# A fused convolution and two-product kernel: block 5 of the convolution gets 20 windows instead of 36, its input is loaded later, and rows go out round by round

## The chip, the cores and the metric

The kernel runs on one core of a Trainium2 chip. The metric is the time of one execution in microseconds (us) of the device. TensorE (PE) multiplies, VectorE (DVE) and ScalarE (ACT) move and scale results out of the accumulation banks, GpSimd (POOL) and SyncE (SP) issue DMA transfers, and the weight loads of TensorE are listed as PEld.

## The reference, cut to what matters

Two steps follow each other. The first is a causal convolution with 7 taps along the sequence; each of 8 heads has its own normalised taps and 24 of the 192 channels. The second is a product of two linear maps, followed by two more linear maps that have no nonlinearity between them.

```python
w = exp(weight - max); w = w / (sum(w) + 1e-9)            # [8 heads, 7 taps]
x_pad = concatenate([zeros((8, 6, 192)), x], axis=1)      # x: [8, 3904, 192]
conv[b, s, h, g] = sum_k w[h, k] * x_pad[b, s + k, h, g]
y = conv.reshape(31232, 192)
a, b = y @ w1, y @ w2                                     # [31232, 1024] each
out = ((a * b) @ w3) @ w_out                              # [31232, 192], float32
```

## The kernel before, in words

**Streams and windows.** The 31,232 tokens are cut into two streams of 15,616 tokens (four sequences each), which sit on the two halves of the 128 partitions. Within a stream the convolution works on windows of 58 new tokens (64 with the six that lap over). A sequence has 68 windows, the last one with 18 tokens, so a stream has 272. `SIZES` cuts them into 12 blocks; `FIRST` holds where each begins, `tok(i)` the token at which window i begins.

**The convolution of a block.** `load_x` brings a block's x in with POOL DMAs, as a whole or in two halves (`halves_of`), cast to bf16 on the way. `zero` clears the six rows ahead of a sequence's first window, where a block holds one. `conv(b, h0, nh)` multiplies nh heads by banded matrices (L290) into one pair of accumulation banks and moves the result to the tile `convo` (L311). `store` writes `convo` to the DRAM tile `rows`, in token order, with two DMAs for each run of windows (48 rows and 10 rows of each window) and one for a sequence's short last window (L330, L334).

**Rounds.** The second step works in rounds of 512 tokens of each stream, 31 in all (numbered 0 to 30, the last with 256). `transposes(R)` brings a round's `rows` back as three DMA transposes into the ring `xT` (L363), which has room for four rounds. `send(last)` issues them on SP for all rounds up to `last` whose tokens are stored. `first_product(R)` (L381, L389, L400) computes both linear maps and their elementwise product into `abT`; `second_product(R, r)` (L434, L439, L446) multiplies by `W_sb` and writes the output for one stream.

**W.** `w3` and `w_out` are multiplied once, ahead of everything that uses them: `w3` goes to DRAM as bf16 (L459), comes back through 16 DMA transposes on SP (L463: 8 for each half of its rows), and `w3_product` (L469, L471) makes the 8 parts of `W_sb` from it. Parts 0 to 3 need the transposes of the first half, parts 4 to 7 those of the second half; the last transpose is read last in each of parts 4 to 7.

**The order.** The whole schedule is written out by hand; each engine and queue works through its own list in order. Blocks 0 to 4 (36 windows) are convolved in a prologue, between the first products of rounds 0 to 2. Block 4 is stored by POOL as far as it is still needed. Then POOL issues, in this order: the load of `w_out`, a two-element copy (`pace`, L559) that waits for one of w3's transposes, and the x of blocks 5 and 6 (L119). PE goes on with the first product of round 3, the eight parts of W, and then the groups: four second products for each stream, into which convolutions are put, then four first products, and so on. A group's loop carries p and the block b = 6 + p that it convolves: three heads behind its second product 1, three behind 3 and two behind 7 (the list `at`). In the group p = 0 block 5 is convolved as well, behind the second products 0, 1 and 2. In later groups the next block's x is loaded behind the first and the second of the four first products, again paced by a two-element copy (L588). The outputs of group 0 go out through POOL's queue, those of later groups through SP's. An SP instruction that waits holds all that stand behind it on SP, and the same holds for POOL.

**What is sent when, before.** Block 5 ends at window 72, token 4136, which covers rounds 4 to 7; block 6 ends at token 6224, which covers rounds 8 to 11. So each block is stored a whole group ahead of the group whose rounds need it.

Of the kernel before, what the change touches and what calls it, by code (L numbers as in the profile page):

```python
# [16 lines left out]
def kernel(  # L17
# [10 lines left out]
    nc = tc.nc  # L28

    B, S, D = x.shape  # L30
    H, K = weight.shape
    G = D // H
    DFF = moe_w1.shape[1]
    JT = DFF // 128
# [4 lines left out]
    CH = 512  # L39
    NR = -(-TS // CH)  # L40
    GROUP = 4
# [4 lines left out]
    WB = -(-S // ST)  # L46
    NWIN = (B // NS) * WB
    LAST = S - (WB - 1) * ST
    SIZES = [6, 4, 8, 10, 8] + [36] * 6 + [20]
    assert sum(SIZES) == NWIN  # L50
    NB = len(SIZES)
    FIRST = [sum(SIZES[:b]) for b in range(NB)]
    PROLOGUE_BLOCKS = 6
    EARLY = SIZES[0] * ST
    MAXN = max(SIZES) // 2

    def tok(i):
        return (i // WB) * S + (i % WB) * ST
# [12 lines left out]
    def banks():  # L71
        p = free.pop(0)
        return p, pairs[:, NS * p:NS * p + NS, :]
# [4 lines left out]
    def drained(p):  # L78
        assert p not in free
        free.append(p)  # L80
# [13 lines left out]
    def halves_of(b):  # L94
        n = SIZES[b] // 2
        return [(FIRST[b], 2 * n)] if 2 * n <= MAXN else [(FIRST[b], n), (FIRST[b] + n, n)]
# [46 lines left out]
    pace = const.tile([1, 2], BF16)  # L143
# [31 lines left out]
    for p0 in (0, Q):  # L175
        nc.gpsimd.affine_select(  # L176
            out=diag[p0:p0 + Q], in_=ones[p0:p0 + Q].to_broadcast([Q, Q + PAD]),
# [3 lines left out]
    for r in range(NS):  # L181
        nc.gpsimd.dma_start(out=xb0[Q * r + PAD:Q * r + Q, 0, :],  # L182
                            in_=x_rows[r * TS:r * TS + ST, :])
# [19 lines left out]
    def warm(n):  # L203
# [14 lines left out]
        out=wall, in0=wall, in1=wmax.unsqueeze(2).to_broadcast([1, H, K]), op=ALU.subtract)  # L218
# [5 lines left out]
        out=wrow, in0=wall, in1=wsum.unsqueeze(2).to_broadcast([1, H, K]), op=ALU.mult)  # L224
# [13 lines left out]
    def band_of(h, r):  # L238
        return Aband[Q * r:Q * r + Q, h // 4, (h % 4) // 2, int(h % 2 != r), :]
# [26 lines left out]
    def segments(c0, n):  # L266
        out = []
        while n:
            m = min(n, Q - c0 % Q)
            out.append((c0 // Q, c0 % Q, m))  # L270
            c0, n = c0 + m, n - m
        return out

    def conv(b, h0, nh, evict=None):
        n = SIZES[b] // 2
        if h0 == 0:
            convo_of[b] = work.tile([128, n, NP, NS, Q], BF16, tag="convo", bufs=2, name="convo")
        convo = convo_of[b]
        p, cps = banks()
        wd = nh * G  # L280

        def view(ps, r):
            return cps[ps, r, 0:n * wd].rearrange("p (w g) -> p w g", g=wd)

        for j in range(nh):
            h = h0 + j
            for c in range(2):
                xb, w0 = xb_of[b][c]
                for r in range(NS):
                    nc.tensor.matmul(  # L290
                        view(slice(Q * c, Q * c + Q), r)[:, :, j * G:(j + 1) * G],
                        band_of(h, r),
                        xb[Q * r:Q * r + Q, w0:w0 + n, h * G:(h + 1) * G],
                        start=True, stop=True)
        src = cps[:, :, 0:n * wd].rearrange("p r (w g) -> p r w g", g=wd)
        o, moves = 0, []
        for k, c0, m in segments(h0 * G, wd):
            moves.append((convo[:, :, k, :, c0:c0 + m].rearrange("p w r g -> p r w g"),
                          src[:, :, :, o:o + m]))
            o += m  # L300
        if h0 + nh == H:
            del xb_of[b]
        if evict == ():
            return p, moves
        if evict == "streams":
            assert nh == H
            return p, [(convo[:, :, :, r, :], src[:, r].rearrange("p w (k g) -> p w k g", k=NP))
                       for r in range(NS)]
        for e, (dst, part) in enumerate(moves):
            f = evict or [nc.scalar.copy]  # L310
            f[e % len(f)](out=dst, in_=part)  # L311
        drained(p)

    stored, sent = [0], [GROUP]

    def store(b, first=0, last=NWIN, queue=nc.sync):
        n = SIZES[b] // 2
        last = min(last, FIRST[b] + 2 * n)
        stored[0] = tok(last) if last < NWIN else TS
        convo = convo_of[b]  # L320
        for c in range(2):
            i0 = FIRST[b] + c * n
            w, end = max(0, first - i0), min(n, last - i0)
            while w < end:
                left = WB - 1 - (i0 + w) % WB
                m = min(end - w, max(1, left))
                src = convo[Q * c:Q * c + ST, w:w + m].rearrange("s w k r g -> s w (k r g)")
                j0 = tok(i0 + w)
                if left == 0:
                    queue.dma_start(out=rows[j0:j0 + LAST, :], in_=src[0:LAST, 0, :])  # L330
                else:
                    dst = rows[j0:j0 + ST * m, :].rearrange("(w s) c -> s w c", s=ST)
                    for s0, s1 in ((0, 48), (48, ST)):
                        queue.dma_start(out=dst[s0:s1], in_=src[s0:s1])  # L334
                w += m
# [23 lines left out]
    def transposes(R, first=0):  # L359
        t0, t1 = max(R * CH, first), min((R + 1) * CH, TS)  # L360
        a = t0 % RING
        for k in range(NP):
            nc.sync.dma_start_transpose(  # L363
                out=xT[k][:, a:a + t1 - t0], in_=rows[t0:t1, k * 128:(k + 1) * 128])
# [45 lines left out]
    def first_product(R, between=None, fts=range(JT), behind_conv=False):  # L410
        if R not in abT_of:
            first_tile(R)
        N = width(R)
        step = CH // N
        for ft in fts[::step]:
            first_part(R, list(range(ft, ft + step)), 0, N)
            if behind_conv and ft == step:
                free[1], free[2] = free[2], free[1]
            if between and ft in between:
                between[ft]()  # L420
# [34 lines left out]
    w3T = const.tile([128, JT, DFF], BF16)  # L455
# [19 lines left out]
    V, A, P = nc.vector.tensor_copy, nc.scalar.copy, nc.gpsimd.tensor_copy  # L475
# [58 lines left out]
    w3_transposes(0, range(JT))  # L534

    def need(R):
        return next(i for i in range(NWIN) if tok(i) >= (R + 1) * CH)

    def send(last):
        while sent[0] <= min(last, NR - 1) and min((sent[0] + 1) * CH, TS) <= stored[0]:  # L540
            transposes(sent[0])
            sent[0] += 1
# [12 lines left out]
        0: seq([(conv, 4, 4, 4)]),  # L555
        3: seq([(pe_transposes, 4)])})
    store(4, need(GROUP - 1) - 1, queue=nc.gpsimd)
    nc.gpsimd.dma_start(out=wo_b, in_=wor)
    P(out=pace, in_=w3T[0:1, 1, DFF - 2:DFF])  # L559
    load_x(5)  # L560
    load_x(6)
    first_product(3)
# [1 line left out]
    def zero(b):  # L564
        for xb, r, w in zero_rows.pop(b, []):
            nc.gpsimd.memset(xb[Q * r:Q * r + PAD, w, :], 0.0)

    def conv_heads(b, heads, f=(nc.vector.tensor_copy,), first=None):
        for j, h in enumerate(heads):
            conv(b, h, 1, (f[j % len(f)],))  # L570
        if heads[-1] == H - 1:
            store(b) if first is None else (store(b, last=first), send(NR), store(b, first))

    slots = (range(0, 3), range(3, 6), range(6, H))
    zero(5)
# [5 lines left out]
    for p, rounds in enumerate(groups):  # L581
        b = PROLOGUE_BLOCKS + p
        order = rounds[-1:] + rounds[:-1] if rounds[-1] == NR - 1 else rounds
        for j, R in enumerate(order if p else ()):
            first_product(R, behind_conv=j == 0 and b <= NB)
            send(R + GROUP)
            if j < 2 and b < NB:
                P(out=pace, in_=abT_of[R][0:1, JT - 1, 1, 0:2])  # L588
                load_x(b, (j,))
        if b < NB:  # L590
            zero(b)
        at = {1: [(b, slots[0])], 3: [(b, slots[1])], 7: [(b, slots[2], (V, A))]}
        if p == 0:
            at = {0: [(5, slots[0], (V, A))], 1: [(5, slots[1], (V, A))],
                  2: [(5, slots[2], (V, A), need(GROUP))], 4: at[1], 5: at[3], 7: at[7]}
        for i, (R, r) in enumerate((R, r) for R in rounds for r in range(NS)):
            second_product(R, r, R == NR - 1 and r == 1, nc.sync if p else nc.gpsimd)
            for c in at.get(i, ()) if b < NB else ():
                conv_heads(*c)
            if p == 0 and i == 2:  # L600
                send(2 * GROUP - 1)
    assert sent[0] == NR


# [28 lines left out]
```

## Time and profile before

| What | Value |
|---|---|
| Median of three runs | 520.85 us (520.66 to 522.95) |
| The profiled execution's own time | 522.15 us |
| Its span, first to last instruction | 520.4 us |
| Mean granted TensorE clock | 0.999 |
| PE busy | 512.2 us, 98% |
| DVE, ACT, POOL busy | 351.9, 330.0, 58.5 us |
| PE on first products (L381) | 3000 matmuls, 319.7 us |
| PE on second products (L434) | 1952 matmuls, 165.0 us |
| PE on the convolution (L290) | 384 matmuls, 17.0 us |
| Moved by DMA | 64.61 MB, mean 124 GB/s |

The busy time of a group is the time in which at least one of its instructions ran; matmuls overlap, so a mean duration times a count is more than the busy time. Idle time stands with the instruction that follows it and what released that instruction. The chain of waits is followed back from the last instruction, at each step to what released it. A DMA's time to landing runs from its issue until its semaphore has been raised in full.

### The profile page before, as it was taken

Reading aid. Unit: us, or ns where it says so; the run is one execution under the profiler, and the core shown is the slowest. Engines: PE = TensorE matmul, PEld = TensorE weight load, DVE = VectorE, ACT = ScalarE, POOL = GpSimd, SP = SyncE. Lnnn points to the kernel's source line nnn. Section 1 sums busy time; section 2 is a strip of 40 time slices with the busy share of each in tenths; the row PEclk is TensorE's granted clock in tenths of the full one; section 3 lists DMA queues with packets and bytes.
Section 4 is the critical chain, followed back from the end, with each engine's and each line's share of the span. In section 5 each row is a group of like instructions: output and inputs, shape, how many; then the busy total and the mean of one; then the engine's idle time right before and its main releaser. Section 6 shows DMA issues by size and latency. Waiting matters only on the chain.

```text
span 520.4 us, 13019 instructions
## 1 busy us (share of the span) xinstructions
PE 512.2 (98%) x5576; PEld 338.0 (65%) x5576; DVE 351.9 (68%) x337; ACT 330.0 (63%) x416; POOL 58.5 (11%) x98
## 2 busy tenths in 40 slices
PE   8999899999999999999999999999999999999997
PEld 4455688445894458845588455884558845599566
DVE  6778644899528995289952899438993199911970
ACT  6887553877438774387743777447774477734762
POOL 8503422030000200003000020001200000000000
PEclk9999999999999999999999999999999999999999
DMA  9979998799747963479644796447824441024004
GB/s 120 165 145 116 153 220 226 158 185 160 141 146 169 115 98 104 141 174 126 85 110 135 167 121 94 116 130 174 104 44 123 139 111 32 17 97 148 2 3 152
DMA packets 133420, 64.61 MB, mean 124 GB/s; under 512 B 90304, under 2 KB 132642, under 8 KB 133298
## 3 DMA queue, kind: packets, MB, share of 16 engines
q1 hardware_dynamic: 94320, 44.06, 36.5%
q0 software_dynamic: 38896, 19.62, 29.0%
q8 instruction: 43, 0.70, 0.6%
q14 instruction: 15, 0.12, 0.1%
q10 hardware_dynamic: 146, 0.10, 0.1%
HBM read 33.25 MB, written 36.52 MB: 134 GB/s over the span
## 4 chain that ended last, share of the span: by engine, by line
PE 87%; SPq 5%; DMA 4%; POOL 3%; issue 0%; ACT 0%; DVE 0%; ACTq 0%
PE pairs L381 53%; PE pairs L434 31%; SPq L463 5%; PE pairs L290 2%; DMA w3rows<-in_moe_w_dram 2%; DMA w3T<-w3rows 2%; POOL xb L119 1%; POOL wd L169 1%; POOL wd L190 1%; PE pairs L469 0%; DMA wall<-in_weight_dram 0%; POOL xb L182 0%; POOL wd L186 0%; POOL xb L172 0%; POOL diag L176 0%
## 5 line engine op out<-in xcount | busy, mean ns | idle before, releaser
L400 DVE TENSOR_TENSOR abT<-asb,pairs 128x1024 bf16<-128x1024 bf16 (+1 forms) x245 | 297.9, 1217 | 52.3 <-ACT asb L389 36.2
L381 PE MATMUL pairs<-xT,wd 64*128 64x512 bf16 (+3 forms) x3000 | 319.7, 371 | 0.7 <-DVE abT L400 0.3
L389 ACT CAST asb<-pairs 128x1024 bf16<-128x1024 f32 (+1 forms) x245 | 247.2, 1009 | 65.7 <-PE pairs L381 65.3
L381 PEld LDWEIGHTS <-wd 64*128 64x128 bf16 x3000 | 160.5, 94 | 154.5 <-issue 2.8
L434 PE MATMUL pairs<-W_sb,abT 128*128 128x192 bf16 x1952 | 165.0, 246 | 0.0
L434 PEld LDWEIGHTS <-abT 128*128 128x128 bf16 x1952 | 159.9, 98 | 7.8 <-issue 7.8
L439 ACT COPY osb<-pairs 128x384 f32<-128x384 f32 x122 | 58.3, 478 | 112.6 <-PE pairs L434 112.6
L311 DVE CAST convo<-pairs 128x864 bf16<-128x864 f32 (+5 forms) x61 | 45.4, 798 | 98.2 <-PE pairs L290 94.0
L119 POOL DMA_DIRECT2D xb<-in_x_dram x42 | 32.2, 782 | 10.6 <-PE pairs L381 5.7
L588 POOL COPY pace<-abT 1x2 bf16<-1x2 bf16 x10 | 1.8, 176 | 239.8 <-DVE abT L400 239.8
L290 PE MATMUL pairs<-xb,Aband 64*64 64x432 bf16 (+5 forms) x384 | 17.0, 284 | 0.0
L311 ACT CAST convo<-pairs 128x864 bf16<-128x864 f32 (+5 forms) x21 | 13.1, 653 | 0.4
L290 PEld LDWEIGHTS <-Aband 64*64 64x64 bf16 x384 | 6.9, 106 | 6.9 <-issue 5.8
L446 POOL DMA_DIRECT2D out_dram<-osb x8 | 6.1, 759 | 18.4 <-ACT osb L439 18.4
L439 DVE COPY osb<-pairs 128x192 f32<-128x192 f32 x1 | 0.4, 357 | 11.1 <-PE pairs L434 11.1
L469 PE MATMUL pairs<-wo_b,w3T 128*128 128x192 bf16 x64 | 5.6, 246 | 1.3 <-DMA w3T<-w3rows 1.3
L469 PEld LDWEIGHTS <-w3T 128*128 128x128 bf16 x64 | 5.2, 98 | 2.0 <-DMA w3T<-w3rows 1.6
L471 ACT CAST W_sb<-pairs 128x192 bf16<-128x192 f32 x8 | 2.6, 319 | 4.3 <-PE pairs L469 4.3
L190 POOL COPY wd<-wd 64x768 bf16<-64x768 bf16 x6 | 4.8, 849 | 0.0
L343 PE MATMUL pairs<-ident,convo 128*128 128x128 bf16 x48 | 3.9, 219 | 0.6 <-DVE convo L478 0.5
L343 PEld LDWEIGHTS <-convo 128*128 128x128 bf16 x48 | 2.9, 97 | 2.4 <-issue 1.6
L206 PE MATMUL pairs<-zeros 128*128 128x512 bf16 x8 | 3.4, 574 | 1.1 <-DVE ones L152 1.1
(52 smaller groups left out, 38.6 us busy)
## 6 DMA issues: line engine op xcount, KB each, us to landing
out_dram<-osb SPq DMA_DIRECT2D x52, 384.0 KB, 2.7
xb<-in_x_dram POOLq DMA_DIRECT2D x18, 432.0 KB, 7.8
rows<-convo SPq DMA_DIRECT2D x8, 648.0 KB, 9.6
out_dram<-osb POOLq DMA_DIRECT2D x8, 384.0 KB, 4.3
w3rows<-in_moe_w_dram POOLq DMA_DIRECT2D x2, 1024.0 KB, 11.7
xb<-in_x_dram POOLq DMA_DIRECT2D x6, 240.0 KB, 5.2
rows<-convo SPq DMA_DIRECT2D x4, 324.0 KB
xT<-rows SPq DMA_TRANSPOSE x81, 2.8
```

The costliest lines, as they stand in the source:

```text
L119: nc.gpsimd.dma_start(out=xb[Q * r:Q * r + Q, w:w + m, :], in_=x_spans(r, i, m))
L190: f(out=wd[i][Q:128, :, cs], in_=wd[i][0:Q, :, cs])
L290: nc.tensor.matmul(view(slice(Q * c, Q * c + Q), r)[:, :, j * G:(j + 1) * G], band_of(h, r), xb[Q * r:Q * r + Q, w0:w0 + n, h * G:(h + 1) ...
L311: f[e % len(f)](out=dst, in_=part)
L343: nc.tensor.transpose(out=tps[:, w, :], in_=convo[:, w, k].rearrange("p r g -> p (r g)"), identity=ident)
L381: nc.tensor.matmul(p[:, r, e * n:e * n + n], wd[i][rs, k, ft * 128:(ft + 1) * 128], xT[k][rs, r0 + c0:r0 + c1], start=(k == 0), stop=(k == ...
L389: nc.scalar.copy(out=asb, in_=pa)
L400: nc.vector.tensor_tensor(out=dst, in0=asb, in1=pb, op=ALU.mult)
L434: nc.tensor.matmul(ops[:, (g - g0) * D:(g - g0) * D + D], ab[:, jt, r, g * 128:(g + 1) * 128], W_sb[:, jt, :], start=(jt == 0), stop=(jt = ...
L439: f(out=osb[:, g0:g0 + per, :].rearrange("p g d -> p (g d)"), in_=ops[:, 0:per * D])
L463: nc.sync.dma_start_transpose(out=w3T[:, gt, j:j + CH], in_=w3rows[j:j + CH, gt * 128:(gt + 1) * 128])
L469: nc.tensor.matmul(wps[:, 0, 0:D], w3T[:, gt, jt * 128:(jt + 1) * 128], wo_b[:, gt, :], start=(gt == 0), stop=(gt == JT - 1))
```

## The change

- `SIZES`: block 5 gets 20 windows instead of 36, and the last block 36 instead of 20. Blocks 6 to 11 all begin 16 windows earlier. Block 5 now ends at window 56, token 3248, which covers rounds 4 and 5; block 6 ends at token 5296 and covers rounds 6 to 9; block 7 covers rounds 10 to 13, and so on. In each group from the second on, the third and the fourth round come from the block that was stored at the end of the group's own second products.
- The copy that paces the x of blocks 5 and 6 reads the 14th of w3's transposes (number 6 of the second half) instead of the 10th (number 2 of the second half).
- Block 5 is convolved two heads at a time, so four times in all instead of eight: six heads behind second product 0 and two behind second product 1.
- `conv_heads` stores every block in two parts with two sends: first the windows that the next round needs, then that round's transposes, then the rest, then the transposes of the rounds that the rest covers, up to four rounds past the group's last. The separate send behind second product 2 of group 0 goes.
- On SP there are 12 DMA issues more than before (48 stores of `rows` at L334 instead of 36); the number of transposes does not change. `need` returns the number of windows where a round has no later window.

```diff
-    SIZES = [6, 4, 8, 10, 8] + [36] * 6 + [20]
+    SIZES = [6, 4, 8, 10, 8, 20] + [36] * 6
...
     def need(R):
-        return next(i for i in range(NWIN) if tok(i) >= (R + 1) * CH)
+        return next((i for i in range(NWIN) if tok(i) >= (R + 1) * CH), NWIN)
...
-    P(out=pace, in_=w3T[0:1, 1, DFF - 2:DFF])
+    P(out=pace, in_=w3T[0:1, JT - 3, DFF - 2:DFF])
     load_x(5)
     load_x(6)
     first_product(3)
...
-    def conv_heads(b, heads, f=(nc.vector.tensor_copy,), first=None):
-        for j, h in enumerate(heads):
-            conv(b, h, 1, (f[j % len(f)],))
+    def conv_heads(b, heads, last, f=(nc.vector.tensor_copy,), nh=1):
+        for j, h in enumerate(heads[::nh]):
+            conv(b, h, nh, (f[j % len(f)],))
         if heads[-1] == H - 1:
-            store(b) if first is None else (store(b, last=first), send(NR), store(b, first))
+            first = min(need(sent[0]), FIRST[b] + SIZES[b])
+            store(b, last=first)
+            send(last)
+            store(b, first)
+            send(last)
...
-        at = {1: [(b, slots[0])], 3: [(b, slots[1])], 7: [(b, slots[2], (V, A))]}
+        ahead = rounds[-1] + GROUP
+        at = {1: [(b, slots[0], ahead)], 3: [(b, slots[1], ahead)],
+              7: [(b, slots[2], ahead, (V, A))]}
         if p == 0:
-            at = {0: [(5, slots[0], (V, A))], 1: [(5, slots[1], (V, A))],
-                  2: [(5, slots[2], (V, A), need(GROUP))], 4: at[1], 5: at[3], 7: at[7]}
+            at = {0: [(5, range(0, 6), ahead, (V, A), 2)], 1: [(5, range(6, H), ahead, (V,), 2)],
+                  4: at[1], 5: at[3], 7: at[7]}
...
-            if p == 0 and i == 2:
-                send(2 * GROUP - 1)
```

## The prediction

> **What bounds the kernel now.** I read the page first (the engines' shares and the chain that ended last), then who waited for whom, then PE, POOL and SP in order of time around the one stall that the change can reach.
>
> ```profile
> span 520.4 us, 13019 instructions
> ...
> PE 512.2 (98%) x5576; PEld 338.0 (65%) x5576; DVE 351.9 (68%) x337; ACT 330.0 (63%) x416; POOL 58.5 (11%) x98
> ...
> PE 87%; SPq 5%; DMA 4%; POOL 3%; issue 0%; ACT 0%; DVE 0%; ACTq 0%
> ```
>
> PE is busy for all but 8.2 us, so only idle PE can be won. Of that, one wait lies where the change works:
>
> ```profile
> POOL pace L559 <- DMA w3T<-w3rows: 8.2, 1, 8.2
> ...
> PE pairs L469 <- DMA w3T<-w3rows: 1.3, 1, 1.3
> ```
>
> PE in order of time shows its place, and the chain of waits what led to it:
>
> ```profile
> 58.76 3.39 PE L469 MATMUL pairs<-wo_b,w3T 128*128 128x192 bf16 x39
> 63.49 2.24 PE L469 MATMUL pairs<-wo_b,w3T 128*128 128x192 bf16 x25 [1.34 <-DMA w3T<-w3rows]
> ```
> ```profile
> 50.26 1.26 SPq L463
> ...
> 53.19 10.26 DMA w3T<-w3rows
> ...
> 68.37 0.67 PE pairs L290 x12
> ...
> 91.05 41.55 PE pairs L381 x384
> ...
> 155.86 41.55 PE pairs L381 x384
> ...
> 397.26 0.43 PE pairs L290 x12
> ```
>
> After 39 of 64 matmuls of W (four whole parts and seven of the fifth) PE stops at 62.15 (58.76 + 3.39) for w3's last transpose, issued at 53.19 and landed 10.26 us later. From there on the chain is PE alone, until the last eviction. The rest of the idle time lies before 50 us or behind the last matmul; the change leaves both alone. So at most 1.34 us can be won here.
>
> **Why that transpose is late.** POOL in order of time, and the landing times (shortest, median, longest) of those transposes of w3 for which the trace gives one:
>
> ```profile
> 49.28 0.18 POOL L559 COPY pace<-w3T 1x2 bf16<-1x2 bf16 x1 [8.23 <-DMA w3T<-w3rows]
> 49.81 6.21 POOL L119 DMA_DIRECT2D xb<-in_x_dram  x8 [0.36 <-PE pairs L381]
> ...
> 67.40 0.25 POOL L566 MEMSET xb<- 6x192 bf16 x1 [0.20 <-DMA xb<-in_x_dram]
> ```
> ```profile
> DMA to landing us min/median/max: 2.7/3.9/5.1
> ```
>
> The pace copy lets x go at 49.8, and the last transpose, issued 3.4 us behind that, takes 10.26 us instead of 2.7 to 5.1. The memset at 67.40 tells when block 5's x (36 windows) was complete: 17.6 us after its first issue, 1 us ahead of its first convolution (68.37).
>
> **The change, part by part.**
>
> *Pace on the 14th transpose.* The transpose issues stand 1.3 us apart; the 14th is the one at 50.26. It lands at 53.0 to 55.4 (2.7 and 5.1 us). I take 53.0, since nothing of x is in flight any more ahead of it. The x then starts at 53.5 (0.53 us from copy to issue, as 49.28 to 49.81), 3.7 us later than before. The last transpose goes out at 52.9 and lands at 55.6 (2.7) to 63.1 (10.26). PE needs it at 62.15. I take an early landing, because it stands ahead of the x loads instead of 3.4 us behind them: gain 1.34 us; at the bad end 0.4 us. Queued behind the copy on POOL are ten x loads, two memsets and eight outputs.
>
> *Block 5's x.* 20 windows instead of 36, 960 KB in place of 1728 KB as written. At the pace of before (17.6 us for 36 windows) it takes 9.8 us and is there at 63.3; from the worst start (55.9) at 65.7. The first convolution comes at 68.37 - 1.34 = 67.0. So this costs nothing; were x later, PE would wait by as much. Block 6's x follows; all 56 windows at the same pace need 27 us, to 81 us, while block 6 is convolved from about 79. Taken against the rate that the loads have once the transposes are gone (next row, last number GB/s), 2.75 MB take 14.4 us, so it is complete by about 70.
>
> ```profile
> 64.00:70.00 6.00, 6.00 (x78) 5.43 (x77) 1.14 (x2) 2.90 (x7) 1.51 (x4) 1.00 1.60 191
> ```
>
> *Memsets.* The two memsets now wait for the eighth of the ten loads, at worst 72 us (38 of 56 windows at the slow pace), ahead of the outputs on POOL. Outputs have five buffers, and the sixth is filled near 80 us, so this is hidden.
>
> *Convolutions.* A block of 36 windows costs PE 0.67 us for three heads, one of 20 windows 0.43 us (rows at 68.37 and 397.26). Block 5 and the last block swap sizes; the sum stays, to within 0.1 us, and only the start of the second group moves, by 0.6 us (0.24 us for three heads, eight heads). The evictions of two heads at once hold 960 columns in place of 864:
>
> ```profile
> L311 DVE CAST convo<-pairs 128x864 bf16<-128x864 f32 (+2 forms) x16 | 12.4, 826 | 19.1 <-PE pairs L290 19.1
> ```
>
> DVE idles 19.1 us ahead of these 16 between 60 and 100 us, and the next use of the same bank pair is four pairs away. Nothing.
>
> *Rows at the border.* This is where a loss could come from: the third and fourth round of each group are now stored and transposed inside the group. Let T be the start of its four first products; each takes 41.55 / 4 = 10.39 us, so the third round must be there at T + 20.8, the fourth at T + 31.2. SP in order of time, behind 76.69 for block 5 and behind 156.92 (T = 155.86) for a whole block, and POOL's x loads in the same group:
>
> ```profile
> 76.69 0.89 SPq L334 DMA_DIRECT2D rows<-convo  x2
> 82.10 3.83 SPq L363 DMA_TRANSPOSE xT<-rows  x3
> 85.98 4.25 SPq L334 DMA_DIRECT2D rows<-convo  x4
> ...
> 95.75 12.68 SPq L363 DMA_TRANSPOSE xT<-rows  x9
> ```
> ```profile
> 156.92 6.18 SPq L334 DMA_DIRECT2D rows<-convo  x4
> 163.15 1.15 SPq L330 DMA_DIRECT2D rows<-convo  x1
> 164.35 0.78 SPq L334 DMA_DIRECT2D rows<-convo  x2
> 165.93 14.83 SPq L363 DMA_TRANSPOSE xT<-rows  x6
> ```
> ```profile
> 169.09 1.70 POOL L119 DMA_DIRECT2D xb<-in_x_dram  x2 [0.79 <-PE pairs L381]
> ...
> 179.00 1.70 POOL L119 DMA_DIRECT2D xb<-in_x_dram  x2 [0.34 <-PE pairs L381]
> ```
>
> First store at T + 1.1. Its rows have landed 5.4 us later (76.69 to 82.10), transposes from T + 6.5 to T + 10.3 (3.83). Even with 10.26 us to landing from the last issue (T + 9.1) the third round is there at T + 19.3. The rest of the store is up to seven DMAs: 9.0 us (156.92 to 165.93) or 9.8 us (85.98 to 95.75) until the next transpose. So the fourth round's three go out from T + 19.3 or 20.1, the last 2.6 us later; it lands between T + 24.6 (2.7) and T + 33.0 (10.26). I take T + 27: the x loads go out at T + 13.2 and T + 23.1, and these transposes fall mostly into the gap. Early, so nothing; at the bad end 1.8 us late at each of five borders (the sixth has no x loads behind it). At the first border SP is still at round 5: store at 72, its transposes from 77.5, round 5's from about 88 to 92, which is T + 3 with T = 89.1 (91.05 less 1.34 and 0.6). There the fourth round lands at T + 29, at worst T + 35. The 12 extra stores lie on SP inside these sums. What SP no longer does is a fourth round's transposes while the second products begin.
>
> A rule of the Trainium skill speaks against this part. "DMA: Bandwidth & Descriptors", section "Queues, rings and completion order", says that each DMA engine takes turns, packet by packet, between the queues that have work. The trace agrees in kind (2.7 us alone, 10.26 us beside x). By the rule, transposes that meet an x load get only every other turn, and whether they meet it decides. If they meet it at every border the sum is that of the bad ends, 530.5; if they go out between the loads it is 519.5.
>
> *The sum:* 1.34 us less, all of it from W. The profiled execution took 522.15 us (span 520.4, 1.75 around it), so 520.8 for it; the median of the runs, 520.85, is 1.3 lower, and from it comes **519.5 us**. About 0.5% (2.6 us) is what a measurement of this kernel can tell from no change, so the forecast is "within".
>
> **The rivals.**
>
> *Nothing won.* The last transpose still lands behind 62.15, say because it is slow for another reason than x, or block 5's x comes after 67.0. For it: the transposes' 5.1 us stands before any of this x. Against: that is far from 10.26. Time 520.4 to 521.5.
>
> *The fourth round is late (slower).* Place: SP at each border, the fourth round's transposes meeting the x load of T + 23.1. For it: the row of 10.26 us, and the first border, which starts 2 us late. Against: the x load of T + 13.2 should be through by then. At the bad ends it costs 3.8 us once and 1.8 us four times, 11 us: 530.5. It decides when the borders together lose over 4.0 us, 0.8 us each, as it then ends above 523.45. If only the first border is late, by 0 to 2 us, the time is 519.5 to 521.5.
>
> *More is won than the one stall.* Something in the records of PE (a busy PE is not PE at its peak) runs faster with lighter DMA traffic. No row shows it; below 518.2.
>
> **How the numbers follow.** The forecast 0.57 (its own range 518.7 to 520.3), nothing won 0.08, late but by no more than 4 us in all 0.17 (519.5 to 523.4), late by more 0.13, more won 0.05. Faster 0.05, slower 0.13, within 0.5% the other 0.82. The range 518.6 to 523.0 leaves out the 0.05 and the 0.13, and little else.
>
> **What the profile after would show.** Right: no idle time ahead of L469, the chain's piece for the last transpose gone or short, the first L119 load of block 5 issued near 53.5, first products of the second group from about 89, no wait of PE on `xT`. Wrong: PE idle ahead of L381 at the third or fourth round of a group, with a transpose as releaser; idle ahead of L290 at 67 us, with x as releaser; a first load far from 53.5.

## The result and the profile after

The changed kernel took 520.0 us (median of 15 executions, 519.75 to 521.65), the kernel before 522.04 us beside it (15 executions, 520.66 to 522.95): a ratio of 0.9972, with 0.9962 to 0.9982 as its 95% interval. The forecast was 519.5 us and no change beyond 0.5%. A second comparison (the run of the changed kernel again, below) gave 520.11 us against 521.58 and a ratio of 0.9995 [0.997, 1.0019]: the ratios go by the means, and there more executions of the changed kernel came out late.

The profiled execution took 520.47 us. Its page, span, engines, and chain by engine:

```profile
span 518.8 us, 13029 instructions
...
PE 512.4 (99%) x5576; PEld 338.7 (65%) x5576; DVE 352.8 (68%) x334; ACT 328.7 (63%) x415; POOL 58.5 (11%) x98
...
PE 95%; DMA 2%; ACT 2%; DVE 1%; issue 0%; ACTq 0%; DVEq 0%
```

SP's and POOL's pieces (8% of the chain before) have gone: with W's wait they led to it, and without it the chain follows PE through that stretch. PE in order of time, from W to the first border:

```profile
58.88 5.45 PE L469 MATMUL pairs<-wo_b,w3T 128*128 128x192 bf16 x64
64.17 2.80 PE L434 MATMUL pairs<-W_sb,abT 128*128 128x192 bf16 x32
66.90 0.81 PE L290 MATMUL pairs<-xb,Aband 64*64 64x240 bf16 x24
...
88.71 31.69 PE L381 MATMUL pairs<-xT,wd 64*128 64x512 bf16 x292
120.84 4.49 PE L381 MATMUL pairs<-xT,wd 64*128 64x512 bf16 x40 [0.45 <-DMA xT<-rows]
```

W's 64 matmuls run in one piece. The new wait is the last row: 0.45 us ahead of the fourth round of the first border (T = 88.71). The chain of waits shows the transfer behind it:

```profile
88.78 23.17 PE pairs L381 x213
111.94 8.86 DMA xT<-rows
...
120.84 10.11 PE pairs L381 x92
```

POOL and SP in order of time:

```profile
52.35 0.18 POOL L559 COPY pace<-w3T 1x2 bf16<-1x2 bf16 x1 [11.20 <-DMA w3T<-w3rows]
52.89 7.38 POOL L119 DMA_DIRECT2D xb<-in_x_dram  x10 [0.36 <-PE pairs L381]
65.95 0.25 POOL L566 MEMSET xb<- 6x192 bf16 x1 [5.68 <-DMA xb<-in_x_dram]
...
101.57 1.74 POOL L119 DMA_DIRECT2D xb<-in_x_dram  x2 [0.36 <-PE pairs L381]
...
111.91 1.70 POOL L119 DMA_DIRECT2D xb<-in_x_dram  x2 [0.34 <-PE pairs L381]
```
```profile
88.90 3.75 SPq L363 DMA_TRANSPOSE xT<-rows  x3
92.75 0.95 SPq L334 DMA_DIRECT2D rows<-convo  x2
95.86 3.73 SPq L363 DMA_TRANSPOSE xT<-rows  x3
99.64 1.01 SPq L334 DMA_DIRECT2D rows<-convo  x2
100.69 0.49 SPq L330 DMA_DIRECT2D rows<-convo  x1
101.23 3.07 SPq L334 DMA_DIRECT2D rows<-convo  x4
108.33 15.58 SPq L363 DMA_TRANSPOSE xT<-rows  x9
```

The x loads of blocks 5 and 6 now start at 52.89. At the border, the last transpose of the fourth round is issued at 111.94, 0.03 us behind the first DMA of the second x load (111.91), and takes 8.86 us.

**Where the time went.** The span is 1.65 us shorter (520.42 to 518.77). By the starts of PE's stages: W took 6.81 us and takes 5.29 (58.76 to 65.57, 58.88 to 64.17): 1.52 less. The second products of group 0 took 25.41 us and take 24.54 (65.57 to 90.98, 64.17 to 88.71): 0.87 less, of which 0.64 comes back in the group that convolves the last block. The border adds 0.62 (the wait of 0.45 and 0.17 around it), the prologue 0.12. And the stretch behind the last matmul, 3.77 us before, is 3.12 us: 0.65 less, which the prediction did not have at all. Sum: 0.12 - 1.52 - 0.87 + 0.64 + 0.62 - 0.65 = -1.66.

### The profile page after: what moved, and what is told of

Same layout as the page of the kernel before. It is cut to its first block, busy times and chain, and to the rows that moved or that the text cites. A ratio compares the mean times of both kernels' runs of the same rounds, so it can differ in the third digit from the quotient of the medians.

```text
span 518.8 us, 13029 instructions
## 1 busy us (share of the span) xinstructions
PE 512.4 (99%) x5576; PEld 338.7 (65%) x5576; DVE 352.8 (68%) x334; ACT 328.7 (63%) x415; POOL 58.5 (11%) x98
## 3 DMA queue, kind: packets, MB, share of 16 engines
q1 hardware_dynamic: 94476, 44.06, 41.7%
## 4 chain that ended last, share of the span: by engine, by line
PE 95%; DMA 2%; ACT 2%; DVE 1%; issue 0%; ACTq 0%; DVEq 0%
PE pairs L381 58%; PE pairs L434 31%; PE pairs L290 3%; DMA xT<-rows 2%; DVE abT L400 1%; PE pairs L469 1%; ACT asb L389 1%; PE pairs L206 1%; PE pairs L343 1%; PE pairs L256 0%; ACT wd L186 0%; ACT convo L311 0%; DVE convo L478 0%; ACT xT L355 0%; PE pairs L509 0%
## 5 line engine op out<-in xcount | busy, mean ns | idle before, releaser
L311 ACT CAST convo<-pairs 128x864 bf16<-128x864 f32 (+4 forms) x20 | 11.8, 626 | 0.4
## 6 DMA issues: line engine op xcount, KB each, us to landing
w3rows<-in_moe_w_dram POOLq DMA_DIRECT2D x2, 1024.0 KB, 11.5
```

## The experiments

Where an edit starts from the kernel before, its text says so; all others start from the changed kernel.

**The pace alone.** The kernel before, with the new pace and nothing else.

```diff
-    P(out=pace, in_=w3T[0:1, 1, DFF - 2:DFF])
+    P(out=pace, in_=w3T[0:1, JT - 3, DFF - 2:DFF])
```

> The kernel before with the pace on the 14th transpose and nothing else. Theory (W's wait goes because x starts behind the transposes; the smaller block only buys time for x): PE idle ahead of L469 0. In the changed kernel 20 windows of x were complete at 62.2 us and 38 at 66.8, so 36 are complete at about 66.4, just ahead of the first convolution at 67.0: idle ahead of L290 0 to 0.5 us. No border wait, so 1.4 us less than before, about 0.4 us less than the changed kernel, ratio 0.997. Rival (the loads keep the pace that the prediction used, 17.6 us for 36 windows): x complete at 70.5, PE idles 3.5 us ahead of L290, ratio 1.003 to 1.004.

It took 521.17 us, ratio 0.9994 [0.9979, 1.001]: nothing that can be told from no change. PE in order of time:

```profile
59.11 5.45 PE L469 MATMUL pairs<-wo_b,w3T 128*128 128x192 bf16 x64
...
67.14 0.37 PE L290 MATMUL pairs<-xb,Aband 64*64 64x432 bf16 x3
67.71 0.70 PE L290 MATMUL pairs<-xb,Aband 64*64 64x432 bf16 x9 [0.20 <-POOL xb L566]
...
101.86 23.49 PE L381 MATMUL pairs<-xT,wd 64*128 64x512 bf16 x216 [0.54 <-DMA xT<-rows]
```

W's wait is gone (1.51 us less for W), but 36 windows of x, started later, come late for the first convolution (67.71), and round 5 comes late by 0.54 at 101.86. By the starts of PE's stages the second products of group 0 lose 0.54 us to before and the first border 0.71, so in this execution the pace alone does not pay.

**The old pace with the smaller block.**

```diff
-    P(out=pace, in_=w3T[0:1, JT - 3, DFF - 2:DFF])
+    P(out=pace, in_=w3T[0:1, 1, DFF - 2:DFF])
```

> The changed kernel with the pace put back on the 10th transpose. Theory: the x loads stand ahead of the last transposes again, the last one takes about 10 us to land, PE idles 1.0 to 1.4 us ahead of L469, and the 0.45 us at the first border stays: ratio 0.999 to 1.001. Rival (the gain comes from the smaller block and its fewer evictions): idle ahead of L469 under 0.3 us and ratio 0.997.

It took 520.53 us, ratio 0.9993 [0.9969, 1.0017]; six of 12 executions took 519.8 to 520.0, the other six 521.0 to 528.9. Against what I held of the pace, the profiled execution (519.93) has no wait in W:

```profile
58.94 5.46 PE L469 MATMUL pairs<-wo_b,w3T 128*128 128x192 bf16 x64
```

Its last transpose was issued at 51.56 and landed at 60.21, 2 us ahead of the 62.2 at which PE needs it. I profiled it a second time, and beside it the kernel before:

> The changed kernel with the pace on the 10th transpose, a second look, unchanged from the first. Theory (in the first look the last transpose landed at 60.2, 2 us ahead of its use, by luck of an early issue): landing between 59 and 63.5, wait ahead of L469 0 to 1.3 us, but the last transposes take 8 us or more to land. Rival (the smaller block's smaller loads disturb the transposes less): 3 us to landing.

> The kernel before, unchanged, for a second look at W's wait. Theory: the last of w3's transposes lands 8 to 10.3 us after its issue, which comes at 51.5 to 53.2 depending on how long SP is held at the transposes ahead of it; PE needs it at 62.2, so the wait ahead of L469 is anywhere from 0 to 1.4 us. Rival: it is a fixed cost, 1.3 us in each execution.

The second profile of the old pace with the smaller block took 519.73, again with no wait (issued at 52.87, landed at 60.28). The kernel before took 521.04, and there W's wait was not 1.34 us:

```profile
58.89 5.76 PE L469 MATMUL pairs<-wo_b,w3T 128*128 128x192 bf16 x64
64.49 1.73 PE L434 MATMUL pairs<-W_sb,abT 128*128 128x192 bf16 x19
```

W took 5.60 us here (58.89 to 64.49) against 5.29 undisturbed, and 6.81 in the first profile. The price of this wait is thus not one number: 0.3 us in this execution, 1.5 in the other. To landing, the last transpose took 10.26 and 9.81 us beside the larger block's x (before, twice) and 8.65 and 7.40 us beside the smaller block's: slow all the same, but somewhat less so. The gap of 1.31 us to the execution beside it (521.04, 519.73) is made up of the tail 0.65, W 0.3, the second products 0.23 and the prologue 0.13.

**The pace far earlier.** If x beside the transposes makes them slow, x let go at the fourth transpose must make W worse.

```diff
-    P(out=pace, in_=w3T[0:1, JT - 3, DFF - 2:DFF])
+    P(out=pace, in_=w3T[0:1, 3, CH - 2:CH])
```

> The changed kernel with the pace on the 4th of w3's transposes, so the x of blocks 5 and 6 goes out as soon as POOL comes to it, near 41 to 42 us, ahead of the whole second half of w3's transposes. Theory (W waits when x is in flight beside w3's last transposes): 2.7 MB of x are in flight until about 60, the eight transposes of the second half land at 2 to 3 us each instead of 1.3, the last between 60 and 66, PE idles 0 to 4 us ahead of L469 (62.2); ratio 0.998 to 1.010, with some runs at a lower clock. Rival (the smaller block alone frees W, wherever its x starts): idle ahead of L469 0, ratio 0.997.

It took 530.01 us, ratio 1.0136 [1.009, 1.0182]. Its waits, and the chain's piece ahead of W's last one:

```profile
PE pairs L469 <- DMA w3T<-w3rows: 3.5, 3, 1.5
...
PE pairs L381 <- DMA xT<-rows: 3.1, 1, 3.1
```
```profile
56.23 10.25 DMA w3T<-w3rows
```

The x loads started at 41.7, and PE then waited three times in W, for transposes that took 9 to 10.5 us. That x is what slows w3's transposes is thus shown. The waits are 6.6 us of the profiled execution's 11.5 us over 520.0 (it took 531.52); most of the rest is the granted clock, told in the last section (PE was busy for 5.37 and 2.80 us at half of it, which by estimate cost 4.1 us).

**Block 5 in three places.** The one-head-at-a-time convolution of before, with the sizes, the pace and the sends of the changed kernel.

```diff
-            at = {0: [(5, range(0, 6), ahead, (V, A), 2)], 1: [(5, range(6, H), ahead, (V,), 2)],
-                  4: at[1], 5: at[3], 7: at[7]}
+            at = {0: [(5, slots[0], ahead, (V, A))], 1: [(5, slots[1], ahead, (V, A))],
+                  2: [(5, slots[2], ahead, (V, A))], 4: at[1], 5: at[3], 7: at[7]}
```

> The changed kernel with block 5's heads one at a time behind the second products 0, 1 and 2, as before the change, instead of two at a time behind 0 and 1. Theory: block 5 is stored near 75 instead of 72, round 5's transposes end 3 us later, block 6's store begins at T + 7 instead of T + 4, and the fourth round of the first border is 2 to 4 us late instead of 0.45; a wait that long also lowers the clock for a while, 1.7 us more; ratio 1.000 to 1.008. Rival (SP has slack there): wait at most 1 us, ratio 0.997 to 0.998.

It took 528.65 us, ratio 1.0123 [1.0093, 1.0153]: 8.65 us more than the changed kernel. PE in order of time, and the windows of the stretch behind (length; busy us and count of PE, PEld, DVE, ACT, POOL; granted clock; DMA share; GB/s):

```profile
123.61 0.39 PE L381 MATMUL pairs<-xT,wd 64*128 64x512 bf16 x2 [2.76 <-DMA xT<-rows]
126.06 4.45 PE L381 MATMUL pairs<-xT,wd 64*128 64x512 bf16 x20 [2.05 <-DMA xT<-rows]
```
```profile
125.10:131.90 6.80, 5.84 (x28) 2.41 (x29) 2.44 (x2) 2.10 (x3) 0.00 (x0) 0.50 0.74 99
```

The chain of waits has the 92 matmuls behind the second wait, which took 10.11 us in the changed kernel:

```profile
126.06 12.98 PE pairs L381 x92
```

Block 5 was stored at 74.77 instead of 72.09 and block 6 from 94.64 instead of 92.75. The fourth round's last transpose went out at 115.00 instead of 111.94 and took 11.01 us. These 2 to 3 us on SP became 4.8 us of waits at the first border, and 6.8 us at half the granted clock, which cost 2.9 us more (12.98 less 10.11): 7.7 of the 8.65. So the border stays nearly in time only because block 5 is convolved in two places, with paired heads. The prediction counted that as nothing on VectorE and did not follow it to SP. The run changes the pairing and the places together; it does not tell them apart.

**All blocks stored whole.** No round is sent ahead of the rest of its block.

```diff
-            first = min(need(sent[0]), FIRST[b] + SIZES[b])
-            store(b, last=first)
-            send(last)
-            store(b, first)
+            store(b)
             send(last)
```

> The changed kernel with every block stored whole ahead of its rounds' transposes, so not round by round. Theory: at the usual border the third round's transposes go out at T + 10 instead of T + 4.5 and land by T + 20 against T + 20.8, the fourth round's land at T + 18 to T + 24, 5 us or more ahead instead of 1.6 to 2.4; at the first border the store begins at T + 1 to T + 2, and the third round is late by 0 to 2 us. So the wait moves from the fourth round to the third; ratio 0.996 to 0.999. Rival (round by round is what keeps the rounds in time): PE waits 1 us or more at the third round of several borders, ratio above 1.000.

It took 522.18 us, ratio 1.0002 [0.9982, 1.0021], some 2 us more than the changed kernel. There are two waits, 1.3 us in all, and they moved to third rounds, as in this row of PE in order of time:

```profile
305.85 20.46 PE L381 MATMUL pairs<-xT,wd 64*128 64x512 bf16 x188 [0.96 <-DMA xT<-rows]
```

So sending round by round is worth about 2 us, of which 0.3 us stands behind the last matmul (last section).

**Block 5 alone stored whole.** SP has fewer DMAs ahead of the first border.

```diff
-            store(b, last=first)
-            send(last)
-            store(b, first)
+            if b > 5:
+                store(b, last=first)
+                send(last)
+                store(b, first)
+            else:
+                store(b)
             send(last)
```

> The changed kernel with block 5 alone stored whole ahead of the transposes of rounds 4 and 5 (the other blocks as in the change). Theory (the first border is late because SP is still at round 5 when block 6 is ready): SP stores block 6 at T + 1 instead of T + 4, the fourth round's last transpose lands near 118 instead of 120.8, the wait of 0.45 us is 0, ratio 0.996 to 0.997. Rival (the x load of T + 23 makes it late whenever SP begins): the last transpose still lands at 120 or later and a wait of 0.2 us or more stays.

It took 520.21 us, ratio 0.9978 [0.9956, 1.0], ten of 12 executions within 520.08 to 520.29. In its profile T is 90.07. SP began block 6's store at T + 1.1 instead of T + 4.0, the fourth round's last transpose landed at T + 29.0 (119.10) instead of T + 32.1, and PE had no wait on a transfer of rows. Yet its usual time is 0.35 us above the changed kernel's usual 519.85. That stands behind the last matmul (last section), not at the border.

**The next x one round later.** The x loads of a group behind its second and third first product.

```diff
-            if j < 2 and b < NB:
+            if 0 < j < 3 and b < NB:
...
-                load_x(b, (j,))
+                load_x(b, (j - 1,))
```

> The changed kernel with the x of the next block loaded behind the second and third first product of a group instead of the first and second, so at T + 23 and T + 33 (T is the start of the group's four first products). Theory (the fourth round was 0.45 us late at the first border because its transposes met the x load): that wait is 0, the fourth round's last transpose lands 4 us or more ahead of its use at the other borders (1.6 to 2.4 us in the changed kernel), 0.4 us less than the changed kernel, ratio 0.996. Rival (it was late because SP came 3 us late to block 6's store): a wait of 0.2 us or more stays at the first border, ratio 0.997.

It took 519.86 us, ratio 0.9968 [0.9954, 0.9982]. POOL and SP in order of time:

```profile
111.88 1.74 POOL L119 DMA_DIRECT2D xb<-in_x_dram  x2 [0.36 <-PE pairs L381]
...
122.21 1.70 POOL L119 DMA_DIRECT2D xb<-in_x_dram  x2 [0.34 <-PE pairs L381]
```
```profile
102.07 1.99 SPq L334 DMA_DIRECT2D rows<-convo  x4
104.98 6.58 SPq L363 DMA_TRANSPOSE xT<-rows  x3
```

With no x at 101.6, the fourth round's transposes start at 104.98 instead of 108.33; the last one, issued at 110.30, ahead of the first x, landed 2.70 us later. There is no wait at the border, and at the next four the fourth round landed by T + 23.4, over 8 us ahead. The first of the three took longer, 6.21 us, with no x in flight: the rest of the block's store, issued just ahead of it on the same queue, landed at 110.4.

**The next x at once.** Both halves behind the first first product.

```diff
-            if j < 2 and b < NB:
+            if j == 0 and b < NB:
...
-                load_x(b, (j,))
+                load_x(b)
```

> The changed kernel with both halves of the next block's x loaded behind the first first product of a group, so at T + 13 in one go. Theory (turns between the queues decide how late the fourth round is): 1.7 MB of x are in flight from T + 15 to about T + 30, the fourth round's last transpose lands at T + 31 to T + 36 against T + 31.2, PE waits 0 to 4 us at each of five borders, 2 to 12 us in all, ratio 1.001 to 1.02. Rival (the transposes get through beside x): at most the 0.45 us of the first border, ratio 0.997.

It took 522.11 us, ratio 1.0011 [0.9986, 1.0036], with executions from 519.78 to 526.78. In the profiled one (524.49) the first border waits twice:

```profile
121.31 0.39 PE L381 MATMUL pairs<-xT,wd 64*128 64x512 bf16 x2 [1.15 <-DMA xT<-rows]
122.98 7.26 PE L381 MATMUL pairs<-xT,wd 64*128 64x512 bf16 x50 [1.28 <-DMA xT<-rows]
```

The next four borders show no wait of note, but have little time to spare: their fourth rounds landed at T + 28.8 to T + 31.7, and PE comes for the last of these transposes at T + 31.7.

**The changed kernel and the later x again.** How often does the first border come late?

> The changed kernel, unchanged, beside the one with later x loads on the same chip. Theory: ratio to before 0.996 to 0.998; in its trace the last transpose of the first border's fourth round lands between 117 and 121.5 against 120.4, so a wait of 0 to 1 us.

> The version with the x loads one first product later, again, beside the changed kernel on the same chip. Theory: no wait for a round at any border, its fourth rounds land 5 us or more ahead, median 0.1 to 0.5 us below that of the changed kernel and fewer slow executions. Rival (the border costs nothing in most executions): the same median within 0.1 us.

The changed kernel took 520.11 us this time, with the ratio given at the start; eight of 12 executions took 519.7 to 520.4 and four 522.7 to 526.5. The profiled one (522.90) was one of the four:

```profile
123.26 2.10 PE L381 MATMUL pairs<-xT,wd 64*128 64x512 bf16 x17 [3.02 <-DMA xT<-rows]
```

The transpose it waited for was issued at 113.12 and took 10.11 us: it landed at T + 34.7 (T = 88.55), close to the prediction's worst case, T + 35. The later x again took 519.86 us, ratio 0.9977 [0.9964, 0.9991]; its profiled execution (520.95) also had a wait:

```profile
121.31 9.03 PE L381 MATMUL pairs<-xT,wd 64*128 64x512 bf16 x82 [0.85 <-DMA xT<-rows]
```

There SP was 1.8 us later than in the first profile (the fourth round's transposes from 106.77 instead of 104.98), the last transpose went out at 113.07, behind the x of 112.00, and took 8.20 us. Of both comparisons, 9 of 27 executions of the changed kernel and 5 of 22 of the later x took over 520.55 us. The medians lie 0.14 and 0.25 us apart. So the later x gains little over the changed kernel, if anything: these executions cannot tell it from no change, and it is not a cure.

## Why the prediction came out as it did

**W's wait: right, with the wrong constancy.** The wait is gone and W takes 1.52 us less, for a forecast of 1.34; the other 0.18 has the size of what the border lost beyond its wait (0.17; the waits of 3.02 and 0.85 us cost 0.18 more each as well). Why a wait costs that much more than its idle time was not tried. The x started at 52.89 (forecast 53.5), w3's last transpose landed at 55.01 (55.6), block 5's x was there at 62.16 (63.3), and PE came for it at 66.90 (67.0). That x makes the transposes slow is shown by the earlier pace. But the forecast took the profile's 1.34 us for the price in every execution, and the second profile of the kernel before had 0.3.

**Which part removes it: not settled.** The forecast gave it all to the pace. The pace alone removed the wait in its profile, and with the smaller block it also stayed away at the old pace, in both profiles, by 2 us. The old pace's six executions of 521.0 us and more were not profiled, so whether the new pace protects some of them stays open.

**The border: the step that failed is "these transposes fall mostly into the gap".** There was no gap. The prediction held that the first x load "should be through by then". At the first border its two DMAs, issued at 101.57 and 102.44, took this long to landing (shortest, median, longest):

```profile
DMA to landing us min/median/max: 7.9/10.4/13.0
```

So it was in flight until 115.40, which is T + 26.7, and the second one went out at T + 23.2. The three transposes of the fourth round, issued at T + 19.6 to T + 23.2, took 7.30, 5.99 and 8.86 us. The sum of SP's stores was near: with an issue at T + 23.2, T + 29 was within reach. But T + 29 leaves 5.8 us and the last transpose took 8.86; it landed at T + 32.1. PE came for it at T + 31.7, as four matmuls of the round run without it (the prediction has T + 31.2). So one of the prediction's own signs of being wrong, PE idle at a fourth round with a transpose as releaser, is there.

The next four borders met x as well: their last transposes took 7.9 to 9.3 us and landed at T + 27.9 to T + 29.6 (forecast T + 27). They were in time partly by luck, because SP issued them at T + 19.6 to T + 20.5, where the prediction's sum has T + 21.9 or later. So the rival "only the first border late by 0 to 2 us" came true in this profile (0.45), was exceeded in the second (3.02), and, by their times, did not come true in most executions. That it is x is shown by the later x (2.70 us to landing, no wait) and by x at once (two waits). By the rule of the Trainium skill cited in the prediction, from "DMA: Bandwidth & Descriptors", section "Queues, rings and completion order", a transpose beside an x load gets only its turns; the trace agrees in kind, with 2.70 us alone and, for the transposes that PE waited for at this border, 8.2 to 11.2 us beside x. But x is not all: with the later x the first transpose of the fourth round took 5.7 to 7.4 us at each of five borders, with no x in flight. The store ahead of it on the same queue is a likely cause, which no run tried.

**Convolutions: "nothing" was a wrong price for the pairing.** The sum of the sizes was right: 0.64 us moved to the last group. But paired heads in two places are what lets SP store block 5 in time; without them the kernel takes 8.65 us more. The step looked at DVE's idle time and left out the queue behind the eviction. The two places also save 0.23 us of second products (24.54 us, and 24.77 with three places).

**What was missing: the end of the kernel.** 0.65 us of the gain stands behind the last matmul. The prediction says of the idle time there that "the change leaves both alone", and gives no reason. These 0.65 and W's 1.52 outweigh the border's 0.62, and so the profiled span lies 1.65 lower for a forecast of 1.34. The right total is in part errors of opposite sign.

**The measured median** is 0.5 us above the forecast, although the profiled gain was larger than forecast: the forecast was set against a median of three (520.85), and the kernel before took 522.04 in the comparison. From 522.04 the same sum gives 520.7, so the nearness to 520.0 owes something to luck here too.

## What to carry to other kernels

A small transfer that the next stage needs should not go out beside a bulk load: the same transpose took under 3 us alone and 8 to 11 us beside x, so the time to spare at each hand-over is to be checked with the second number, and it is better to move the bulk load than to count on a gap. A hand-over with a spare time near zero does not cost a fixed amount: it splits the executions into those that wait and those that do not, so one profile gives neither its price nor its absence. An eviction that ends earlier on an idle engine can be worth much where a queue behind it feeds a tight hand-over.

## What the runs showed of the hardware

**The end of the program came out shorter with 12 more DMAs.** The events of the program's closing line show SP going through eight DMA semaphores in a fixed order. Its instructions on SP (count; shortest, median, longest in ns; first and last start), of before, after, and block 5 alone stored whole:

```profile
L628 SPq EVENT_SEMAPHORE  x11: 17/28/28, 516.9 to 520.4; - x11
```
```profile
L632 SPq EVENT_SEMAPHORE  x11: 17/28/28, 515.9 to 518.7; - x11
```
```profile
L635 SPq EVENT_SEMAPHORE  x11: 17/28/28, 516.9 to 519.9; - x11
```

The last matmuls end at 516.66, 515.66 and 516.52 by the chains, so the tails are 3.77, 3.12 and 3.46 us. SP issues 36, 48 and 46 stores at L334 in these three, so 0, 12 and 10 DMAs more than before; all blocks stored whole has 34, and a tail of 3.42. The tail was 3.77 in every profile with the count of before and 3.11 to 3.13 in those with 12 more. In the traces the count moves the last four DMAs to other places among the eight semaphores: before, SP goes through five checks behind the last landing, after through one, which makes 0.27 us of the 0.65. But all blocks stored whole has seven, and still a shorter tail than before, so the checks are not the whole reason. The rest is at SP's next instruction, a DRAIN: before, it starts 0.35 us behind the last check and takes 124 ns, after it starts 0.04 us behind and takes 7 ns (rows of before and after):

```profile
L628 SPq DRAIN  x3: 7/7/124, 519.5 to 519.9; - x3
```
```profile
L632 SPq DRAIN  x3: 7/7/7, 517.9 to 518.2; - x3
```

What makes this difference stays open, and no run adds DMAs and nothing else.

**A wait of PE can cost more than itself.** After the two waits of x at once, the granted clock (the third number from the end) halves:

```profile
119.00:124.00 5.00, 2.58 (x24) 1.12 (x22) 2.46 (x3) 1.66 (x3) 0.00 (x0) 1.00 1.51 144
124.10:127.40 3.30, 3.30 (x18) 1.46 (x16) 2.08 (x2) 1.33 (x2) 0.00 (x0) 0.50 1.38 151
127.50:131.00 3.50, 3.50 (x36) 1.90 (x34) 2.46 (x3) 2.75 (x3) 0.00 (x0) 1.00 0.23 19
```

By the trace's record of the clock the stretch at 0.50 lasted 3.41 us here. With the pace far earlier there were two, of 6.83 us (behind three waits of 3.5 us in all) and of 3.41 us (behind one of 3.08), and with block 5 in three places one of 6.83 us (2.76 and 2.05). After the single wait of 3.02 us in the second profile of the changed kernel, the clock stayed whole:

```profile
123.30:127.00 3.70, 3.70 (x36) 2.00 (x37) 2.19 (x2) 2.74 (x3) 0.00 (x0) 1.00 0.74 148
```

The Trainium skill, "TensorE: Matmul & The Clock Gate", section "Part 1: The HAM clock gate (the "warmup" mystery)", says that the clock falls to half after an idle window of about 3.4 us (3413 ns), and that the windows run freely. The lengths of these stretches, one and two times 3.41 us, agree. The threshold does not: two waits of 1.15 and 1.28 us were enough, and one of 3.02 was not. What in these waits decides is not settled by the runs. Nor is every such stretch behind a wait on a transfer: the profiled execution of block 5 alone stored whole (521.67, its others mostly 520.2) had one in the prologue, in which the changed kernel's profile shows none:

```profile
8.60:11.90 3.30, 3.30 (x53) 1.92 (x53) 1.27 (x4) 1.66 (x3) 3.30 (x5) 0.50 1.01 108
```
